# Decay attention and a gated convolution on one core: all 707 pieces of work in another written order

## The chip, the core and the metric

The kernel runs on one core of a Trainium2 chip. The metric is device time in microseconds of one execution. The kernel before takes 206.38 us, the median of three runs (206.31 to 206.44). A core has five engines with a queue of instructions each, and the queues run in order: TensorE (PE; its weight loads are listed apart as PEld), VectorE (DVE), ScalarE (ACT), GpSimd (POOL) and SyncE (SP), which here issues every transfer.

## The reference

Two stages. The first is a causal linear attention with a decay per head, over 4 batches, 8 heads, 768 positions and a head width of 64; `lam` holds the decay of each head. In blocks of positions, with a running state of 64x64 per head:

```
intra = (q_b @ k_b^T) * lam^(i-j), lower triangle
out_b = intra @ v_b + (q_b * lam^(i+1)) @ state
state = lam^block * state + (k_b * lam^(block-1-i))^T @ v_b
```

The second takes the result as `x` (4 batches, 768 tokens, 512 channels):

```
gate_pre[t] = sum over k < 5 of conv_w[k] * x[t - 4 + k]      (per channel)
out = (sigmoid(gate_pre) * (x @ w_val)) @ w_out
```

`q`, `k`, `v` and `lam` are float32; `w_val`, `conv_w` and `w_out` arrive as float64.

## The kernel before

A **chunk** is 128 positions of two batches, all heads; there are 12, numbered 0 to 11, and 0 to 5 share one running state, as do 6 to 11. Two chunks are a **unit** for the convolution. The work is cut into 707 **pieces**, each a few instructions on one engine, that the functions below register with `plan.add`. The order in which pieces are emitted, and so the order of every engine's queue, is written out by hand in the string `ORDER` (from line 32). `Plan.run` walks through it and emits each piece. What follows a colon in `ORDER` names the buffers that the piece takes: `u0` to `u3` are four banks of PSUM that most results pass through, `lq0` to `lq2` and `lv0` to `lv2` are the landing places of loads. Semaphores that a layer below derives from the data keep the result right in any order that `Plan.run` accepts; the order alone decides who waits.

```
    def run(self):
        done = set()
        for piece in ORDER.split():
            name, _, takes = piece.partition(":")
            k = self.at[name]
            assert k not in done and done.issuperset(self.work[k][3]), name
            done.add(k)
            self.takes = takes.split(",") if takes else []
            self.work[k][2]()
```

The names that the later sections use, with chunk number i (or unit n), engine and line:

- On the transfer queue: `ld.i.0` loads q and k of a chunk transposed (1 MB, `lq`, L337), `ld.i.2` loads v and k (1 MB, `lv`, L337), `wv.u` and `wo.u` load halves of the two weight matrices as raw 64-bit words (1 MB each, L355), `cv` the convolution's weights (20 KB, L370), `o...` stores a result (256 KB, L851).
- Weights are turned from float64 into a high and a low float32 part by integer steps: `.e .n .s .w .v` on DVE (L261 to L293), `.r .m .h` on ACT, `.l` on POOL (L303).
- Attention on PE: `s.i.u` scores (L460 and L470), `ia.i.u` scores times v (`xp`, L525 and L510), `in.i.u` q times state (also into `xp`, L536 and L547), `st.i` k times v (L564 and L572). These are short matmuls of 64 or 128 columns, 32 to 64 instructions a piece. Beside them: `m.i.b.u` multiplies scores by the decay mask (DVE, L483 and L490), `kd.i` scales k, `up.i` updates the state (DVE, L581), `fd.i` decays it (POOL, L584), `x.i` copies `xp` out of PSUM (ACT, L634), `xh.i` and `xl.i` split it into high and low parts.
- Second stage on PE: `v.i.f` and `V.n.f` are the value products (`vp`, L732), 12 matmuls of 256 columns for one chunk or of 512 for a whole unit, and `p.i.b.j.u` the output products (`op`, L841), 6 matmuls of 512 columns. `t.` are the five taps of the convolution (ACT then DVE, L704 and L706), `sg` the sigmoid, `pb.i.u` copies `vp` out of PSUM (ACT, L773), `ap`, `hh`, `hl` multiply and split, `ev` copies the output out of PSUM (ACT, L848).
- `f.0` (L206) is a matmul of zeros that nothing reads, there to keep PE occupied.

Loads wait on SP for their landing place: `ld.5.2` for example takes `lv1`, which chunk 3 holds until `ia.3.1` and `st.3` have read it.

Of the kernel before, what the change touches and what calls it, by code (L numbers as in the profile page):

```python
# [33 lines left out]
ld.1.2:lv1 wv.1:g1 m.0.0.1:A1 m.0.1.1 ia.0.1 f.0:u2 wv.0.0.e:val0 ld.2.0:lq2 wv.0.0.n ld.4.0:lq0 cv wv.0.0.r
wv.0.1.e:val1 ld.2.2:lv2 wv.0.0.m:u3 wv.0.0.s wv.0.0.w xh.0:xs0 wv.0.0.v wo.0:hs0 xl.0 st.0:u2 qd.1.1:qd0 up.0.0
wv.0.1.r wv.0.0.h s.1.0:s0 m.1.1.0:A0 s.1.1:u0,u1 m.1.0.0 dc wv.0.0.l v.0.0:u3 m.1.0.1:A1 x.0:x0 qd.1.0 ld.3.0:lq1
fd.0.0 kd.1.0 wo.1:hs1 m.1.1.1 wv.0.1.n ia.1.0:xp0 ia.1.1 wv.0.1.m:u2 ld.4.2:lv0 wv.1.0.e:val2 in.1.0 st.1:u0 wv.0.1.s
wv.0.1.w wv.0.1.v wv.0.1.h ld.3.2:lv1 wv.1.0.n s.2.0:s0 wv.1.1.e:val3 s.2.1:u1,u2 up.1.0 xh.1 wv.0.1.l v.0.1
m.2.0.0:A0 m.2.1.0 wv.1.0.m:u0 xl.1 wv.1.0.w wv.1.0.r hi.0 pb.0.0:val0 m.2.0.1:A1 wv.1.0.s cv.e qd.2.0:qd1 wv.1.0.v
qd.2.1 wv.1.1.n x.1 wv.1.1.r cv.r s.4.0:s0 cv.n v.1.0:u3 v.1.1 wv.1.0.h wv.1.1.s wv.1.1.m:u0 m.2.1.1 wv.1.1.w wv.1.1.v  # L40
ia.2.0:xp0 ia.2.1 wv.1.0.l cv.m m.4.1.0:A0 kd.2.0 wv.1.1.h fd.1.0 wo.0.0.n:val1 cv.s in.2.0 x.2:x1 pb.1.0:val2
wv.1.1.l m.4.0.0 st.2:u1 wo.0.0.e wo.0.0.r up.2.0 qd.4.0:qd0 cv.w cv.v xh.2:xs1 wo.1.1.e:val3 t.0.0.0:u2,g0 s.3.0:s0
xl.2.0 wo.0.0.m:u0 v.0.2:u3 m.3.0.0:A1 ld.6.2:lv2 v.0.3 pb.0.1 t.0.0.1 kd.3.0 t.0.0.2 xl.2.1 t.0.0.3 wo.0.0.w qd.4.1
ld.5.0:lq2 wo.0.0.s t.0.0.4 v.1.2:u1 sg.0.0 qd.3.1:qd1 v.1.3 v.2.2:u3 v.2.3 pb.1.1 wo.1.1.n fd.2.0 wo.0.0.v m.3.1.0
wo.1.1.m:u2 wo.1.1.r ld.6.0:lq0 st.3:u0,u1 wo.0.0.h qd.3.0 ia.3.0:xp0 in.3.0 wo.1.1.w wo.1.1.s wo.1.1.v wo.0.0.l hi.1
s.5.0:s0 kd.4.0 v.2.0:u2 up.3.0 in.3.1 wo.0.1.e:val1 wo.0.1.r fd.3.0 wo.1.1.h wo.0.1.n wo.0.1.m:u0 wo.0.1.s wo.1.1.l
up.3.1 fd.3.1 ia.3.1 v.2.1 x.3 xh.3 xl.3.1 ia.4.0:xp0 t.0.1.0:u1 ld.5.2:lv1 wo.0.1.w xl.3.0 pb.2.0:val3 m.5.1.0:A1
m.5.0.0 wo.0.1.v pb.2.1 wo.0.1.h wo.0.1.l s.6.0:s0 st.4:u0,u2 qd.5.1:qd1 kd.6.0 t.0.1.1 t.0.1.2 t.0.1.3 in.4.0 up.4.0
fd.4.0 t.0.1.4 sg.0.1 v.3.0:u3 kd.5.0 v.3.2:u0 qd.5.0 in.4.1 ia.4.1 ld.7.2:lv0 t.0.3.0:u1 t.0.3.1 up.4.1 t.0.3.2
x.4:x2 t.0.3.3 t.0.2.0:u2 kd.5.1 v.3.3 pb.3.1:val1 t.0.2.1 t.0.2.2 xh.4:xs0 ld.7.0:lq1 ia.5.0:xp0 in.5.0 t.0.2.3  # L50
fd.4.1 st.5:u0 up.5.0 v.3.1 pb.3.0 t.0.3.4 xl.4.1 in.5.1 sg.0.3 t.0.2.4 ap.1.0 ap.0.0 sg.0.2 ap.1.1 xl.4.0
wo.1.0.e:val2 wo.1.0.r v.4.0:u0 v.4.2:u3 wo.1.0.n wo.1.0.m:u1 ap.0.1 v.4.1 wo.1.0.s hh.1.1:hs0 wo.1.0.w pb.4.0:val0
hh.1.0 hl.1.1 wo.1.0.v m.6.1.0:A0 v.4.3 m.6.0.0 t.1.1.0:u2,g1 t.1.1.1 wo.1.0.h ia.5.1 st.6:u0,u1 up.6.0 x.5 s.7.0:s0
ia.6.0:xp0 hl.1.0 p.1.1.0.0:u0 t.1.1.2 hh.0.1:hs1 hh.0.0 t.1.1.3 pk.6 wo.1.0.l p.1.1.0.1 pb.4.1 qd.6.1:qd0 t.1.1.4
qd.6.0 t.1.3.0:u3 sg.1.1 t.1.3.1 t.1.3.2 t.1.3.3 t.1.3.4 ev.1.1.0:o0 o.1.1.0 xh.5 in.6.1 hi.2 ia.6.1 p.1.0.0.0:u2
fd.6.0 x.6:x0 t.1.0.0:u0 hl.0.0 sg.1.3 hl.0.1 p.1.0.0.1 up.6.1 ld.11.2:lv1 t.1.0.1 t.1.0.2 t.1.0.3 t.1.0.4
p.0.1.0.0:u1 ev.1.0.0:o1 p.0.1.0.1 t.1.2.0:u3 m.7.0.0:A1 t.1.2.1 t.1.2.2 t.1.2.3 m.7.1.0 sg.1.0 xl.5.0 p.0.0.0.0:u2
p.0.0.0.1 xl.5.1 v.5.0:u0 ld.8.0:lq2 t.1.2.4 ev.0.1.0:o2 o.1.0.0 xh.6:xs1 qd.7.0:qd1 t.2.3.0:u1,g0 v.5.1 ap.3.0
ld.8.2:lv2 ev.0.0.0:o0 sg.1.2 pb.5.0:val2 ap.3.1 ap.2.0 qd.7.1 kd.7.1 ia.7.0:xp0 in.7.0 kd.7.0 ap.2.1 hh.2.1:hs0
st.7:u2,u3 fd.6.1 v.5.2:u0 v.5.3 hh.2.0 t.2.3.1 t.2.3.2 up.7.0 s.8.0:s0 in.7.1 t.2.3.3 t.2.1.0:u2 t.2.3.4 hh.3.0:hs1  # L60
ia.7.1 hh.3.1 hl.2.0 sg.2.3 pb.5.1 p.2.0.0.0:u1 t.2.0.0:u0 t.2.1.1 ld.9.2:lv0 t.2.1.2 t.2.0.1 fd.7.0 up.7.1 hl.2.1
t.2.0.2 t.2.0.3 kd.8.0 p.2.0.0.1 ev.2.0.0:o1 t.2.0.4 sg.2.0 p.2.1.0.0:u3 kd.8.1 t.2.2.0:u1 t.2.1.3 p.2.1.0.1 t.2.1.4
o.2.0.0 sg.2.1 m.8.0.0:A0 o.0.0.0 t.2.2.1 t.2.2.2 t.2.2.3 t.2.2.4 ev.2.1.0:o1 o.0.1.0 ap.4.0 ap.5.0 ld.9.0:lq0 hl.3.1
hi.3 hl.3.0 x.7 p.3.0.0.0:u0 p.3.0.0.1 p.3.1.0.0:u2 t.3.0.0:u3,g1 xh.7 p.3.1.0.1 o.2.1.0 ia.8.0:xp0 sg.2.2 ap.4.1
t.3.0.1 hh.4.0:hs0 t.3.0.2 t.3.0.3 qd.8.1:qd0 fd.7.1 qd.8.0 in.8.0 ev.3.0.0:o0 hl.4.0 hh.4.1 hl.4.1 ev.3.1.0:o2
t.3.0.4 st.8:u1,u0 up.8.0 xl.6.0 ap.5.1 p.4.0.0.0:u2 m.8.1.0 t.3.1.0:u1 xl.7.1 p.4.0.0.1 fd.8.0 in.8.1 t.3.1.1 t.3.1.2
ia.8.1 t.3.1.3 ev.4.0.0:o1 o.4.0.0 ld.10.0:lq1 s.9.0:s0 m.9.1.0:A1 p.4.1.0.0:u2 sg.3.0 x.8:x1 p.4.1.0.1 xl.6.1
hh.5.0:hs1 t.3.2.0:u3 ev.4.1.0:o1 up.8.1 t.3.2.1 t.3.1.4 xl.7.0 V.3.0:u0 t.3.2.2 sg.3.1 m.9.0.0 t.3.3.0:u2 hl.5.0
t.3.2.3 t.3.2.4 sg.3.2 t.3.3.1 t.3.3.2 V.3.1:u1 ld.11.0:lq2 ld.10.2:lv2 V.3.2:u3 qd.9.1:qd1 qd.9.0 qd.10.1:qd0 t.3.3.3
kd.9.1 fd.8.1 kd.9.0 apw.3.0 xh.8:xs0 hhw.3.0:hs0 kd.11.1 o.3.0.0 t.3.3.4 apw.3.1 hhw.3.1 ia.9.0:xp0 hlw.3.0:val1  # L70
hlw.3.1 in.9.0 st.9:u0,u1 sg.3.3 hh.5.1 apw.3.2 hhw.3.2 V.3.3:u2 up.9.0 fd.9.0 kd.11.0 kd.10.0 in.9.1 ia.9.1 s.10.0:s0
apw.3.3 hhw.3.3 qd.10.0 hlw.3.2:val3 p.7.0.0.0:u0 hlw.3.3 x.9 hi.4 t.4.1.0:u3,g1 hl.5.1 p.5.1.0.0:u2 p.5.1.0.1
ev.5.1.0:o0 m.10.0.0:A0 up.9.1 p.7.0.0.1 t.4.1.1 o.5.1.0 t.4.1.2 t.4.1.3 t.4.1.4 sg.4.1 kd.10.1 ia.10.0:xp0 fd.9.1
st.10:u1,u2 xh.9 in.10.0 up.10.0 m.10.1.0 ev.7.0.0:o0 o.7.0.0 qd.11.0:qd1 p.6.1.0.0:u3 p.6.1.0.1 in.10.1 ia.10.1
o.4.1.0 x.10:x2 t.4.0.0:u0 xh.10:xs1 s.11.0:s0 qd.11.1 ev.6.1.0:o0 o.6.1.0 fd.10.0 up.10.1 st.11:u1 m.11.0.0:A1
fd.10.1 t.4.0.1 t.4.0.2 ia.11.0:xp0 in.11.0 up.11.0 m.11.1.0 o.3.1.0 xl.9.0 p.6.0.0.0:u2 xl.9.1 t.4.0.3 t.4.0.4
p.6.0.0.1 ev.6.0.0:o1 sg.4.0 p.7.1.0.0:u3 t.4.2.0:u1 t.4.2.1 in.11.1 ia.11.1 x.11 t.4.2.2 xh.11 t.4.2.3 p.7.1.0.1
t.4.2.4 xl.8.1 xl.8.0 t.4.3.0:u2 sg.4.2 t.4.3.1 t.4.3.2 V.4.0:u0 apw.4.0 t.4.3.3 V.4.2:u1 t.4.3.4 hhw.4.0:hs0
ev.7.1.0:o0 sg.4.3 hlw.4.0:val0 V.4.1:u3 apw.4.1 apw.4.2 hhw.4.1 hlw.4.1 hi.5 t.5.1.0:u2,g0 t.5.1.1 hhw.4.2 V.4.3:u0
apw.4.3 hlw.4.2:val2 hhw.4.3 p.5.0.0.0:u3 t.5.1.2 p.5.0.0.1 p.9.0.0.0:u1 xl.10.0 hlw.4.3 p.9.0.0.1 t.5.1.3 t.5.1.4  # L80
t.5.3.0:u0 ev.5.0.0:o2 o.5.0.0 sg.5.1 ev.9.0.0:o2 p.8.0.0.0:u3 p.8.0.0.1 o.9.0.0 xl.11.0 xl.10.1 xl.11.1 V.5.1:u2
t.5.3.1 t.5.0.0:u1 t.5.3.2 t.5.3.3 t.5.3.4 sg.5.3 ev.8.0.0:o2 t.5.0.1 t.5.0.2 t.5.0.3 t.5.0.4 sg.5.0 p.9.1.0.0:u0
t.5.2.0:u3 o.8.0.0 apw.5.1 hhw.5.1:hs1 t.5.2.1 t.5.2.2 p.9.1.0.1 ev.9.1.0:o2 t.5.2.3 t.5.2.4 sg.5.2 o.7.1.0 V.5.0:u1
hlw.5.1:val1 V.5.3:u0 apw.5.0 o.9.1.0 apw.5.3 hhw.5.3 hlw.5.3:val3 p.8.1.0.0:u2 p.8.1.0.1 V.5.2:u3 hhw.5.0 ev.8.1.0:o0
o.8.1.0 hlw.5.0 p.10.1.0.0:u0 o.6.0.0 apw.5.2 hhw.5.2 hlw.5.2 p.11.1.0.0:u1 p.11.0.0.0:u2 p.11.0.0.1 ev.11.0.0:o2
o.11.0.0 p.11.1.0.1 ev.11.1.0:o0 o.11.1.0 p.10.1.0.1 ev.10.1.0:o1 o.10.1.0 p.10.0.0.0:u3 p.10.0.0.1 ev.10.0.0:o2
o.10.0.0 p.11.1.1.0:u2 p.11.1.1.1 ev.11.1.1:o0 o.11.1.1
"""


# [812 lines left out]
```

## Time and profile before

| | |
|---|---|
| median of 3 runs | 206.38 us (206.31 to 206.44) |
| the profiled execution's own time | 206.52 us |
| its span, from the first to the last instruction | 204.7 us |
| PE, PEld busy | 97%, 84% of the span |
| DVE, ACT, POOL busy | 75%, 56%, 56% |
| TensorE clock granted | full (mean 1.00) |
| transfers | 36.15 MB, mean 177 GB/s; 360 to 429 GB/s in the slices from about 5 to 46 us |

The span is 1.8 us shorter than the execution; that share lies outside the program's instructions. PE's busy share is a modelled one, since matmuls overlap; the chain of waits and the waits by engine tell more. The first 45 us are the dense part: the loads of the weights and of the first six chunks stream without a break, and DVE and ACT turn the weights into two parts beside the attention's own work.

### The profile page before, as it was taken

The numbers are of one execution on the slowest core, as the hardware profiler recorded it, in microseconds if no ns is written. First come the engines' busy times: TensorE is split into PE (matmuls) and PEld (weight loads), VectorE is DVE, ScalarE is ACT, GpSimd is POOL, SyncE is SP. The second block draws the span as 40 slices with busy tenths as digits, with TensorE's granted clock in tenths as the row PEclk, the third lists the DMA queues.
The fourth block names the chain that finished last, engine by engine and source line by source line (L and its number), as shares of the span: only waits on it lengthen the run. The fifth ranks groups of instructions, "written<-read, shape, count | busy, mean of one in ns | idle before, by whom it ended". The sixth has DMA issues, their size and how long they took to land.

```text
span 204.7 us, 7451 instructions
## 1 busy us (share of the span) xinstructions
PE 197.6 (97%) x3312; PEld 171.6 (84%) x3312; DVE 154.1 (75%) x240; ACT 114.3 (56%) x218; POOL 115.4 (56%) x113
## 2 busy tenths in 40 slices
...
GB/s 175 426 429 419 422 424 423 421 360 27 195 51 362 8 3 118 373 232 3 297 297 29 203 400 122 3 3 152 8 106 0 0 3 102 102 51 14 93 127 78
DMA packets 7952, 36.15 MB, mean 177 GB/s; under 512 B 1136, under 2 KB 1392, under 8 KB 4336
## 3 DMA queue, kind: packets, MB, share of 16 engines
...
q8 instruction: 26, 0.43, 0.9%
q14 instruction: 6, 0.05, 0.1%
...
## 4 chain that ended last, share of the span: by engine, by line
PE 87%; DMA 9%; SPq 2%; issue 0%; ACT 0%; ACTq 0%
PE op L841 33%; PE vp L732 33%; DMA lq<-in_qkv 9%; PE xp L510 5%; PE s L470 5%; PE xp L547 5%; PE st L572 4%; SPq L337 1%; PE xp L525 1%; PE s L460 1%; PE st L564 1%; PE xp L536 1%; SPq L355 0%; PE so L460 0%; ACT o L848 0%
## 5 line engine op out<-in xcount | busy, mean ns | idle before, releaser
L706 DVE SCALAR_TENSOR_TENSOR acc<-x,conv_sb,acc 128x512 f32<-128x512 f32 x96 | 71.5, 753 | 7.8 <-ACT acc L704 5.7
L732 PE MATMUL vp<-x_hi,wv_hi 128*128 128x256 f32 (+1 forms) x144 | 47.1, 327 | 0.0
L732 PE MATMUL vp<-x_hi,wv_lo 128*128 128x256 f32 (+1 forms) x144 | 45.9, 319 | 0.3 <-POOL wv_lo L303 0.3
L732 PE MATMUL vp<-x_lo,wv_hi 128*128 128x256 f32 (+1 forms) x144 | 45.8, 318 | 0.0
L841 PE MATMUL op<-wo_hi,hs 128*128 128x512 f32 x96 | 30.4, 398 | 0.0
L848 ACT COPY o<-op 128x512 f32<-128x512 f32 (+1 forms) x25 | 14.3, 570 | 28.5 <-PE op L841 24.2
L732 PEld LDWEIGHTS vp<-x_hi,wv_hi 128*128 128x128 f32 x144 | 27.3, 190 | 2.8
L732 PEld LDWEIGHTS vp<-x_hi,wv_lo 128*128 128x128 f32 x144 | 27.4, 190 | 2.4 <-POOL wv_lo L303 0.5
L732 PEld LDWEIGHTS vp<-x_lo,wv_hi 128*128 128x128 f32 x144 | 27.4, 190 | 1.9
L677 POOL TENSOR_TENSOR x_lo<-x,x_hi 128x512 fp32r<-128x512 f32 x20 | 25.8, 1311 | 4.7 <-ACT x_hi L666 4.7
L584 POOL TENSOR_TENSOR sdec<-state,qdec_c 128x512 f32<-128x512 f32 x17 | 18.4, 1080 | 9.2 <-DVE state L581 9.2
L814 POOL TENSOR_TENSOR hs<-g,hs 128x512 fp32r<-128x512 f32 x12 | 15.4, 1294 | 13.6 <-ACT hs L803 13.6
L420 POOL TENSOR_TENSOR qd<-lq,qdec_c 128x512 f32<-128x512 f32 (+1 forms) x18 | 22.6, 1272 | 0.0
L841 PEld LDWEIGHTS op<-wo_hi,hs 128*128 128x128 f32 x96 | 17.7, 188 | 4.0
L841 PE MATMUL op<-wo_hi,h_hi 128*128 128x512 f32 (+1 forms) x52 | 20.0, 385 | 0.0
L841 PE MATMUL op<-wo_hi,h_lo 128*128 128x512 f32 (+1 forms) x52 | 19.6, 377 | 0.0
L704 ACT ACTIVATE acc<-x,conv_sb 128x512 f32<-128x512 f32 x24 | 16.7, 696 | 5.1 <-DVE state L581 3.6
L841 PE MATMUL op<-wo_lo,h_hi 128*128 128x512 f32 (+1 forms) x52 | 19.5, 375 | 0.0
L841 PE MATMUL op<-wo_lo,hs 128*128 128x512 f32 x48 | 18.9, 393 | 0.0
L803 ACT CAST h_hi<-vp 128x512 fp32r<-128x512 f32 x12 | 6.9, 587 | 21.0 <-DVE vp L778 21.0
L581 DVE TENSOR_TENSOR state<-st,sdec 128x512 f32<-128x512 f32 x17 | 11.7, 688 | 8.8 <-PE xp L547 6.4
L778 DVE TENSOR_TENSOR vp<-vp,g 128x512 f32<-128x512 f32 x12 | 8.3, 698 | 11.9 <-PE vp L732 11.9
...
## 6 DMA issues: line engine op xcount, KB each, us to landing
lq<-in_qkv SPq DMA_DIRECT2D x12, 1024.0 KB, 7.8
lv<-in_qkv SPq DMA_DIRECT2D x12, 1024.0 KB, 8.0
...
w_raw<-in_w_val SPq DMA_DIRECT2D x2, 1024.0 KB, 12.6
w_raw<-in_w_out SPq DMA_DIRECT2D x2, 1024.0 KB, 17.6
...
lam_bc<-in_lam SPq DMA_DIRECT2D x1, 4.0 KB, 1.6
```

The source lines that it names most:

```text
L420: nc.gpsimd.tensor_tensor(out=s["qd"][:, hs, ms], in0=lds[i]["qT"][:, u].rearrange("p h (m i) -> p h m i", m=2)[:, :, ms], in1=qdec[:, hs, ...
L470: nc.tensor.matmul(sp[b][rows(m), k, :], t["kT"][rows(b), u, h, ms], t["qT"][rows(b), u, h, ms], start=True, stop=True,)
L510: nc.tensor.matmul(s["xp"][rows(hh), b ^ m, b, g, :], lds[i]["v"][rows(m), b, h * D : (h + 1) * D], s["A"][rows(m), b, h, :], start=b == 0 ...
L581: nc.vector.tensor_tensor(out=state, in0=s["st"][m], in1=sdec, op=ALU.add)
L584: nc.gpsimd.tensor_tensor(out=sdec, in0=state, in1=qdec_c[:, :, n - 1 : n].to_broadcast([P, H, D]), op=ALU.mult)
L677: nc.gpsimd.tensor_tensor(out=s["x_lo"][:, ts], in0=s["x"][:, ts], in1=s["x_hi"][:, ts].bitcast(F32), op=ALU.subtract)
L704: nc.scalar.mul(to, src, w)
L706: nc.vector.scalar_tensor_tensor(out=to, in0=src, scalar=w, in1=to, op0=ALU.mult, op1=ALU.add)
L732: nc.tensor.matmul(to, w[:, ct, fs], xx[:, ct], start=n_mm == 0, stop=n_mm == 3 * NT - 1)
L814: (nc.vector if direct else nc.gpsimd).tensor_tensor(out=to, in0=x["h", j, fs], in1=x["to", j, fs].bitcast(F32), op=ALU.subtract)
L841: nc.tensor.matmul(s["op", b, j][:, cols], hh, w[:, ft, cols], start=ft == 0 and n == 0, stop=ft == NT - 1 and n == 2,)
L848: nc.scalar.copy(s["o", b, j][:, cols], s["op", b, j][:, cols])
```

## The change

Only the string `ORDER` changes; no piece, engine, size or buffer count does, and every engine issues as many instructions as before. The new order keeps the same outline. The string's first line, before and after:

```
-ld.0.0:lq0 dm.0 dm.1 qe ld.0.2:lv0 kd.0.0 s.0.0:s0 kd.0.1 m.0.0.0:A0 s.0.1:u0,u1 m.0.1.0 ia.0.0:xp0 wv.0:g0 ld.1.0:lq1
...
+dm.0 dm.1 dc ld.0.0:lq0 qe f.0:u0 ld.0.2:lv0 kd.0.1 s.0.1:u0,u1 m.0.1.1:A0 s.0.0:s0 wv.0:g0 kd.0.0 m.0.0.1 m.0.1.0:A1
...
```

Three places, as the built programs list their instructions.

The transfer queue (SP) near its start, from the first half of `w_val` on, before and then after. `lq` and `lv` are loads of chunks, `w_raw` of weights, `conv_raw` of the convolution's weights.

```order
L355 DMA w_raw<-in_w_val 128x2048
L337 DMA lq<-in_qkv 128x2048
L337 DMA lv<-in_qkv 128x2048
L355 DMA w_raw<-in_w_val 128x2048
L337 DMA lq<-in_qkv 128x2048 x2
L370 DMA conv_raw<-in_conv_w 128x40
L337 DMA lv<-in_qkv 128x2048
L355 DMA w_raw<-in_w_out 128x2048
```

```order
L355 DMA w_raw<-in_w_val 128x2048
L337 DMA lq<-in_qkv 128x2048
L337 DMA lv<-in_qkv 128x2048
L370 DMA conv_raw<-in_conv_w 128x40
L355 DMA w_raw<-in_w_val 128x2048
L337 DMA lq<-in_qkv 128x2048 x2
L355 DMA w_raw<-in_w_out 128x2048
L337 DMA lv<-in_qkv 128x2048
```

The convolution's weights (`cv`) now stand ahead of the second half of `w_val` and of `ld.2.0`, and the first half of `w_out` (`wo.0`) ahead of `ld.2.2`.

DVE at the start, before and then after: the masks of chunk 0 (`A`), then the first steps on the weights (`w_em`, `w_v`).

```order
L483 TENSOR_TENSOR A<-s,mask_c 128x512 x2
L483 TENSOR_TENSOR A<-so,mask_c 128x512 x2
L261 TENSOR_SCALAR w_em<-w_raw 128x512
L268 TENSOR_SCALAR w_em<-w_raw 128x512
L261 TENSOR_SCALAR w_em<-w_raw 128x512
L281 SCALAR_TENSOR_TENSOR w_em<-w_raw,w_em 128x512
```

```order
L483 TENSOR_TENSOR A<-so,mask_c 128x512 x2
L483 TENSOR_TENSOR A<-s,mask_c 128x512 x2
L261 TENSOR_SCALAR w_em<-w_raw 128x512 x2
L268 TENSOR_SCALAR w_em<-w_raw 128x512 x2
L281 SCALAR_TENSOR_TENSOR w_em<-w_raw,w_em 128x512
```

The second half of the heads is masked first, and a fourth step on the weights (`wv.0.1.n`) stands ahead of the sign step of the first block (`wv.0.0.s`).

PE around chunk 4, between `v.2.1` and the next value products, before and then after: `ia.4.0`, `s.6.0`, `st.4`, `in.4.0` are the four short pieces.

```order
L732 MATMUL vp<-x_hi,wv_lo 128x256
L510 MATMUL xp<-A,lv 64x64 x16
L470 MATMUL s<-lq 64x64 x32
L572 MATMUL st<-lv 64x64 x32
L547 MATMUL xp<-qd,state 64x64 x16
L732 MATMUL vp<-x_hi,wv_hi 128x256
```

```order
L732 MATMUL vp<-x_hi,wv_lo 128x256
L510 MATMUL xp<-A,lv 64x64 x16
L547 MATMUL xp<-qd,state 64x64 x16
L572 MATMUL st<-lv 64x64 x32
L470 MATMUL s<-lq 64x64 x32
L732 MATMUL vp<-x_hi,wv_hi 128x256
```

The same four stand there; `in.4.0` and `st.4` come ahead of `s.6.0`. A little earlier, the run `st.3`, `ia.3.0`, `in.3.0`, `s.5.0` becomes `ia.3.0`, `st.3`, then the product `v.2.3`, then `in.3.0`, `s.5.0`, `in.3.1`; `v.2.0` now stands between `in.3.1` and `ia.3.1`, which were neighbours. `f.0` moves from behind `ia.0.1` to the head of PE's queue, ahead of the first scores.

## Rows read from the trace of the kernel before

**Rows 1.** The page: span, and busy time by engine.
```profile
span 204.7 us, 7451 instructions
PE 197.6 (97%) x3312; PEld 171.6 (84%) x3312; DVE 154.1 (75%) x240; ACT 114.3 (56%) x218; POOL 115.4 (56%) x113
```

**Rows 2.** Instructions in time, PE, to 24 us: start, length, what, idle before and releaser.
```profile
10.76 1.12 PE L206 MATMUL fill<-zero 128*128 128x512 f32 x2
12.04 1.15 PE L564 MATMUL st<-lv 128*64 128x64 f32 x32
13.64 1.16 PE L460 MATMUL s<-lq 64*128 64x128 f32 x16 [0.45 <-DMA lq<-in_qkv]
20.78 1.15 PE L564 MATMUL st<-lv 128*64 128x64 f32 x32
22.45 1.16 PE L460 MATMUL s<-lq 64*128 64x128 f32 x16 [0.52 <-DMA lq<-in_qkv]
```

**Rows 3.** Instructions in time, DVE, from 8 to 12 us.
```profile
8.62 1.28 DVE L483 TENSOR_TENSOR A<-so,mask_c 128x512 f32<-128x512 f32 x2
11.51 0.42 DVE L268 TENSOR_SCALAR w_em<-w_raw 128x512 int32<-128x512 int32 x1
```

**Rows 4.** The chain that ended last: start, length, what; here the issue of ld.2.0.
```profile
4.34 18.07 DMA lq<-in_qkv
```

**Rows 5.** Instructions in time, SP: issues of ld.1.2 and of ld.5.2.
```profile
3.32 0.45 SPq L337 DMA_DIRECT2D lv<-in_qkv  x1
50.01 0.33 SPq L337 DMA_DIRECT2D lv<-in_qkv  x1
```

**Rows 6.** DMA issues from 3.2 to 3.4 us: KB each, us to landing.
```profile
lv<-in_qkv SPq DMA_DIRECT2D x1, 1024.0 KB, 14.4
```

**Rows 7.** The chain that ended last, from 49 to 58 us.
```profile
49.90 1.63 PE vp L732 x12
51.53 0.62 PE xp L510 x32
52.15 0.99 PE s L470 x53
53.14 0.10 issue
53.24 0.39 PE s L470 x10
55.08 3.06 PE vp L732 x24
```

**Rows 8.** The chain that ended last, from 71 to 74 us.
```profile
71.09 0.62 PE xp L510 x32
71.71 0.93 PE st L572 x64
72.64 0.93 PE s L470 x64
73.58 0.47 PE xp L510 x32
```

**Rows 9.** DMA queues of the page, then those of 50.9 to 51 us: packets, MB, share.
```profile
q8 instruction: 26, 0.43, 0.9%
...
q8 instruction: 1, 0.02, 59.1%
```

**Rows 10.** The same from 46.4 to 46.5 us.
```profile
q8 instruction: 1, 0.02, 89.3%
```

**Rows 11.** Instructions in time near chunks 3 and 4, PE, DVE and ACT.
```profile
45.60 0.65 PE L547 MATMUL xp<-qd,state 64*64 64x64 f32 x32
46.38 0.69 DVE L581 TENSOR_TENSOR state<-st,sdec 128x512 f32<-128x512 f32 x1 [0.64 <-POOL x L641]
49.97 1.08 ACT L634 COPY x<-xp 128x512 f32<-128x512 f32 x2 [0.66 <-PE xp L510]
51.07 1.05 ACT L666 CAST x_hi<-x 128x1024 fp32r<-128x1024 f32 x1
52.65 1.06 ACT L773 COPY val<-vp 128x512 f32<-128x512 f32 x2
```

More of the change, by code (lines that the diff above doesn't have):

```diff
@@ L32 @@
 ORDER = """
-ld.0.0:lq0 dm.0 dm.1 qe ld.0.2:lv0 kd.0.0 s.0.0:s0 kd.0.1 m.0.0.0:A0 s.0.1:u0,u1 m.0.1.0 ia.0.0:xp0 wv.0:g0 ld.1.0:lq1
[L34 to L87, printed above, removed]
+dm.0 dm.1 dc ld.0.0:lq0 qe f.0:u0 ld.0.2:lv0 kd.0.1 s.0.1:u0,u1 m.0.1.1:A0 s.0.0:s0 wv.0:g0 kd.0.0 m.0.0.1 m.0.1.0:A1
@@ new lines @@
+m.0.0.0 ia.0.0:xp0 ld.1.0:lq1 ld.1.2:lv1 ia.0.1 wv.0.0.e:val0 cv wv.1:g1 wv.0.1.e:val1 wv.0.0.n qd.1.1:qd0 wv.0.1.n
+wv.0.0.r wv.0.0.s ld.2.0:lq2 ld.4.0:lq0 wo.0:hs0 wv.0.0.m:u2 wv.0.0.w wv.0.0.v xh.0:xs0 xl.0 ld.2.2:lv2 wv.0.0.h
+wv.0.0.l wv.0.1.r st.0:u3 x.0:x0 qd.1.0 s.1.1:u0,u1 up.0.0 s.1.0:s0 fd.0.0 v.0.0:u2 ld.3.0:lq1 m.1.0.0:A1 m.1.1.0
+m.1.0.1:A0 ia.1.0:xp0 m.1.1.1 wo.1:hs1 cv.e ld.4.2:lv0 ia.1.1 in.1.0 wv.0.1.m:u3 kd.1.0 st.1:u0 wv.0.1.s wv.0.1.w
+wv.0.1.v wv.0.1.h ld.3.2:lv1 cv.n cv.m wv.1.0.n:val2 wv.1.1.e:val3 up.1.0 wv.0.1.l s.2.0:s0 wv.1.0.e xh.1 xl.1
```

49 lines of the change are left out of this document (added).

## The prediction

> **What bounds the kernel now.** I read the page's busy times first. PE is busy for 197.6 of 204.7 us [rows 1]; the other engines have at least 50 us to spare, so what counts is PE's stretch from its first real matmul to its last, and in it the moments in which PE stands still or runs at less than its usual pace. Next the instructions in time on PE. Up to 22.45 us the loads set the pace: `s.1.0` waits 0.45 us for `ld.1.0`, `s.2.0` 0.52 us for `ld.2.0` [rows 2], which was issued at 4.34 and landed 18.07 us later, at 22.41 [rows 4]. From then on the chain of waits consists of PE alone, piece on piece, and a wait is visible only as a piece that takes longer than its like. There is one place of that kind. The four short pieces around chunk 4 start at 51.53 and the next product at 55.08, so they take 3.55 us [rows 7]. The same kinds (`ia`, `st`, `s`, `ia`) around chunk 6 take 0.62 + 0.93 + 0.93 + 0.47 = 2.95 us [rows 8]. So 0.60 us is lost there, nearly all in `s.6.0`: 0.99 + 0.10 + 0.39 = 1.48 us, where `s.7.0` takes 0.93. The chain marks a part of it as issue, time in which no semaphore is waited for.
>
> What else PE fetches at that moment is in the DMA queues: PE's instructions come in 26 packets, 0.43 MB, so 16 KB each [rows 9]. One of them starts between 50.9 and 51.0 us, right behind the issue of `ld.5.2` at 50.01 into a queue that had run empty [rows 5], and lasts 0.591 x 16 x 0.1 = 0.95 us, to about 51.9. The hole in `s.6.0` ends at 53.24, 1.3 us after that packet. I read the hole as an instruction page that came late; the rows show the coincidence, not the cause.
>
> **The change part by part.** Work and durations stay, so PE's sum changes only by its starts, its switches and its waits. I count against the profiled execution (206.52 us, of which 204.7 are the span) and carry the difference over to the median of 206.38.
>
> *Start, to 22.45 us: +0.05.* Three edits, all behind a load. `f.0` (1.12 us) [rows 2] moves ahead of the first scores, which wait for their load anyhow. In its place comes a wait: DVE now masks the second half first, so `ia.0.0` needs all four masks, which are done at 9.90 [rows 3]. `ia.0.0` and `ia.0.1` need about 2 us, so `st.0` again starts at about 12.0 and ends at 13.2; `s.1` waits for its load until 13.64 either way. Cover 0.4 us. One more weight step (0.42 us) [rows 3] ahead of `wv.0.0.s` makes the low part of the first weight block up to 0.4 us later, and with it `v.0.0` and all up to `st.1`, which ended at 21.93 [rows 2]: 22.3 at the latest, still under the landing at 22.41. What remains is the landing itself: the 20 KB of `cv` now lie ahead of `ld.2.0`. From the landing of `ld.1.2` (3.32 + 14.4 = 17.7) [rows 5, 6] to 22.41 two transfers of 1,024 KB take 4.7 us, 2.35 each, so 20 KB cost 0.05 us by bytes. Bounds 0 and, as its rows are small, 0.3; I take 0.05. `wo.0` ahead of `ld.2.2` puts that load 2.35 us later, near 29.8; its first reader on PE is due about 30.2. I cost it at nothing; if the cover were gone, each 0.1 us that it is late costs 0.1.
>
> *Switches between short and long matmuls: +0.35.* `v.2.3` is cut out of a row of products and `v.2.0` put between `in.3.1` and `ia.3.1`, so from 22 us on PE has one more stretch of products and one more of short pieces. A product of its own takes 1.63 us, two in a row 3.06, so 1.43 for one more in a row [rows 7]: 0.20 a stretch. A short `xp` piece takes 0.62 next to a product and 0.47 among short ones [rows 8]: 0.15. Bounds 0 (if the other places regain it) and 0.4.
>
> *The hole around chunk 4: -0.60.* The packet is asked for by PE's place in its own stream. Ahead of `ia.3.1` stands now the long `v.2.0` in place of the short `in.3.1`, so the request can go out during a product that lasts 1.6 us, more ahead of `ld.5.2`, whose issue still waits for `ia.3.1`. I count the hole and the small wait with it as gone. Bounds 0 and -0.60; nearer to -0.60, since a request 0.3 us earlier is enough.
>
> *Two new waits: +0.10 and +0.15.* `in.3.1` follows `s.5.0` at once, and needs `up.3.0`, which needs `in.3.0`. In the trace `in.3.0` starts at 45.60 and `up.3.0` is done at 47.07, 1.47 us later [rows 11]; PE gets to `in.3.1` after 0.47 + 0.93 = 1.40. With the hand-over between engines some 0.1 us. And `st.4` writes a bank that `pb.2.1` empties, which ACT does behind `x.3` and `xh.3`: from the end of `ia.3.1` at 49.90 these end at 52.1, and one copy of 1.06 / 2 more [rows 11] makes 2.7 us; PE's way from there is `v.2.1`, `ia.4.0`, `in.4.0`, 1.63 + 0.62 + 0.47 = 2.72. A tie, with a hand-over on ACT's side: 0.15. In the order before, `s.6.0` lay between. Bounds 0 and 0.3 each. Behind a waiting `st.4` stands PE's queue alone.
>
> *Everything behind 56 us: 0.* The outline is kept, PE's last pieces are again two halves of the last output, and the tail behind them (copy, store) is the same.
>
> Sum: 0.05 + 0.35 - 0.60 + 0.10 + 0.15 = +0.05, so 206.4.
>
> **A rule that speaks against the hole's cause.** The rows show 26 packets of 16 KB and, once, PE short of instructions [rows 7, 9]. The Trainium skill, "Runtime: NRT & Kernel Launch", section "Instruction fetch mechanics", says that the sequencer fetches the next block of 256 instructions while it executes the current one, and that crossing a block is mostly hidden. The block size agrees with the packets here; the hole, if it is one of fetching, does not agree with hidden. By that rule the hole has another cause and stays as it is: that is the third rival below.
>
> **The rivals.**
>
> *Faster, 205.9.* `ld.1.2` landed 4.1 us after `ld.1.0` (13.6, by the wait of `s.1.0`) [rows 2], where the next two took 2.35 each: 1.7 us of the load stream went astray. If that does not recur, `ld.2.0` is there at 20.7, and `s.2.0` starts when PE gets there, about 22.15: -0.30, and the 0.05 of `cv` with it. If also the two new waits do not show: -0.25. Sum +0.05 - 0.35 - 0.25 = -0.55. For it: both waits are near ties. Against: the packets of PE's instructions and the loads meet again in the same first 20 us.
>
> *Slower, 207.2.* The late page strikes harder. The four short pieces still stand in a row and `ld.5.2` is still issued when `ia.3.1` ends. PE reaches the point at which it ran dry (53.24 less a hole of 0.3) after the same work, some 0.4 us later by the switches and the wait of `in.3.1`, so near 53.3; the packet must end 1.3 us ahead of that, by 52.0 us. Where packets meet other traffic they last longer: 0.893 x 1.6 = 1.43 us at 46.4 us against 0.95 [rows 9, 10]. A packet that starts as late as before (50.95), half a microsecond later for the load ahead of it, and lasts 1.43, ends at 52.9 and costs 0.9, of which `st.4` hides its 0.15. Sum +0.05 + 0.75 = +0.8. It decides as soon as the packet ends later than 52.0. For it: the places are close. Against: the earlier request.
>
> *The hole stays, 206.7.* 53 of the 64 instructions of `s.6.0` should take 53/64 x 0.93 = 0.77 us, and the 54th came 1.09 after the first: 0.32 is the hole without the rest. It stays as it is, since the packet goes out as late as before, and the sum is +0.05 + 0.32 = +0.37, less a little that the wait at `st.4` shares with it. The rule above gives the same.
>
> **How the numbers follow.** Forecast 206.4 (its own range 206.0 to 206.8): chance 0.54. Faster rival 0.20, slower rival 0.16, hole stays 0.10. A measurement of this kernel tells about 0.2% from no change, so 205.97 and 206.79 are the borders. Of the forecast 0.02 lies beyond each border, of the last rival 0.02 beyond the upper one. Faster 0.20 + 0.02 = 0.22, slower 0.16 + 0.02 + 0.02 = 0.20, same 0.58. The range 205.8 to 207.2 leaves out about a third of the faster rival and half of the slower one, 0.15.
>
> **What would show it.** Right: `s.2.0` starts at 22.3 to 22.6 with a wait for its load; the four short pieces around chunk 4 take about 3.0 us plus a wait at `st.4` of at most 0.3, with no piece of the chain marked issue; PE's last matmul ends within 0.4 us of 201.7. Wrong: `s.2.0` at 22.2 or earlier (faster rival); an instruction packet that ends later than 52.0 and a hole behind it (slower rival); a new wait anywhere behind 56 us, where I expect none, which would make the whole sum wrong.

## The result and the profile after

The changed kernel takes 208.01 us (median of 4 runs, 207.96 to 208.24). The kernel before, run beside it on the same chip, takes 206.41 (206.31 to 206.45). The ratio is 1.0081, with a 95% interval of 1.0069 to 1.0093. So the change costs 1.6 us, where 206.4 was forecast and 207.2 was the upper end of the range.

The head of the page of the changed kernel, answering to [rows 1]:

```profile
span 206.2 us, 7454 instructions
...
PE 198.6 (96%) x3312; PEld 171.9 (83%) x3312; DVE 153.0 (74%) x240; ACT 114.8 (56%) x218; POOL 114.8 (56%) x113
...
PE 86%; DMA 8%; DVE 2%; issue 1%; ACT 1%; SPq 1%; POOL 1%; ACTq 0%
```

The span grew by 1.5 us and PE's busy time by 1.0 (197.6 to 198.6). The last line, the shares of the chain of waits, has two entries to look into. DMA stood at 9% before too, but there all of it was the load of `s.2.0` at the start; of the 8% here the page puts 4% down to `out<-o`, the store of a result. And "issue" has gone from 0% to 1%.

The chain from 22 us on, answering to [rows 2] (columns: start, length, what):

```profile
22.40 1.16 PE s L460 x16
...
24.46 1.64 PE vp L732 x12
26.10 0.90 issue
27.00 1.16 PE s L470 x64
```

`s.2.0` starts at 22.40, 0.05 us ahead of before and inside the forecast 22.3 to 22.6, though not with the forecast wait: its load has landed at 22.27, just when TensorE is through with `st.1`. But `s.4.0` starts at 27.00, 0.90 us after TensorE was free, where before it started at 26.06 with no wait. The view calls this gap "issue", and the view of instructions in time names the last product as what `s.4.0` waited for. Neither tells the cause: what `s.4.0` needs is its bank, and that is free when VectorE has masked both halves of `s.2.0` (`m.2.0.0`, `m.2.1.0`). VectorE and GpSimd at that moment, instructions in time:

```profile
22.39 0.69 DVE L581 TENSOR_TENSOR state<-st,sdec 128x512 f32<-128x512 f32 x1 [0.64 <-PE st L564]
22.99 1.52 DVE L261 TENSOR_SCALAR w_em<-w_raw 128x512 int32<-128x512 int32 x1
24.43 1.28 DVE L672 TENSOR_TENSOR x_lo<-xp,x_hi 128x512 fp32r<-128x512 f32 x2
25.63 1.27 DVE L483 TENSOR_TENSOR A<-s,mask_c 128x512 f32<-128x512 f32 x2
...
22.95 2.71 POOL L413 TENSOR_TENSOR qd<-lq,qdec_c 128x512 f32<-128x512 f32 x2
```

The two masks (L483) end at 26.90, and `s.4.0` starts 0.1 us later. Ahead of them stand `wv.1.0.e` (L261) and `xl.1` (L672), which the change has moved there. And `wv.1.0.e` takes 1.52 us. In the kernel before, the same step ran with GpSimd idle and took 0.43:

```profile
20.00 0.43 DVE L261 TENSOR_SCALAR w_em<-w_raw 128x512 int32<-128x512 int32 x1 [1.02 <-DMA w_raw<-in_w_val]
```

There the same two masks ended at 24.95, 1.1 us before TensorE came to `s.4.0`:

```profile
23.66 1.29 DVE L483 TENSOR_TENSOR A<-s,mask_c 128x512 f32<-128x512 f32 x2
...
26.06 1.16 PE L470 MATMUL s<-lq 64*64 64x64 f32 x64
```

Around chunk 4, answering to [rows 7]:

```profile
52.92 0.62 PE xp L510 x32
53.55 0.47 PE xp L547 x32
54.01 1.13 PE st L572 x61
55.15 0.01 PE s L470
55.15 0.05 PE st L572 x3
55.20 0.93 PE s L470 x63
56.14 1.87 PE vp L732 x14
```

The four short pieces now take 56.14 - 52.92 = 3.22 us instead of 3.55. The hole in `s.6.0` is gone; `st.4` takes 0.26 more than its like [rows 8], 0.15 of it in one gap between two of its instructions.

The second loss lies behind 96 us (the same view, the pieces that matter):

```profile
97.75 0.33 SPq L337
...
98.13 7.43 DMA out<-o
...
105.64 0.60 ACT o L848
...
106.28 3.04 PE op L841 x12
```

The store `o.0.0.0` was issued at 98.13, right behind the load `ld.9.2` (97.75), and landed only 7.43 us later. The copy `ev.2.0.0` needs the buffer that it empties, and `p.3.0.0.0` needs the bank which that copy empties. TensorE stands still for 0.32 us.

In the starts of TensorE's pieces against the kernel before, the delay is -0.05 at `s.2.0`, +0.94 at `v.1.0`, +1.06 at `v.3.3` (60 us), +1.45 at `p.4.1.0.0` (116 us) and +1.53 at the end (203.22 against 201.69).

### The profile page after: what moved, and what is told of

Same layout as the page of the kernel before. It is cut to its first block, busy times and chain, and to the rows that moved or that the text cites. A ratio compares the mean times of both kernels' runs of the same rounds, so it can differ in the third digit from the quotient of the medians.

```text
span 206.2 us, 7454 instructions
## 1 busy us (share of the span) xinstructions
PE 198.6 (96%) x3312; PEld 171.9 (83%) x3312; DVE 153.0 (74%) x240; ACT 114.8 (56%) x218; POOL 114.8 (56%) x113
## 4 chain that ended last, share of the span: by engine, by line
PE 86%; DMA 8%; DVE 2%; issue 1%; ACT 1%; SPq 1%; POOL 1%; ACTq 0%
PE vp L732 34%; PE op L841 29%; PE xp L510 5%; PE xp L547 5%; DMA w_raw<-in_w_val 4%; PE s L470 4%; PE st L572 4%; DMA out<-o 4%; PE xp L525 2%; PE st L564 1%; PE xp L536 1%; POOL wv_lo L303 1%; SPq L337 1%; PE s L460 1%; ACT o L848 0%
## 5 line engine op out<-in xcount | busy, mean ns | idle before, releaser
L420 POOL TENSOR_TENSOR qd<-lq,qdec_c 128x512 f32<-128x512 f32 (+1 forms) x18 | 22.6, 1263 | 0.0
L711 ACT ACTIVATE g<-acc 128x512 f32<-128x512 f32 x24 | 14.4, 599 | 9.8 <-DVE acc L706 9.6
L581 DVE TENSOR_TENSOR state<-st,sdec 128x512 f32<-128x512 f32 x17 | 11.7, 687 | 7.3 <-PE st L572 3.6
```

Source lines behind the costliest of these rows:

```text
L420: nc.gpsimd.tensor_tensor(out=s["qd"][:, hs, ms], in0=lds[i]["qT"][:, u].rearrange("p h (m i) -> p h m i", m=2)[:, :, ms], in1=qdec[:, hs, ...
L581: nc.vector.tensor_tensor(out=state, in0=s["st"][m], in1=sdec, op=ALU.add)
L711: nc.scalar.activation(xu[un]["g"][:, ct].rearrange("p u (b i) -> p b u i", b=NB2), xu[un]["acc", ct].rearrange("p b (u i) -> p b u i", u= ...
```

## Experiments

All edits but three are in the order string alone (the two runs with an extra GpSimd step and the measurement at the end have code as well). The diffs show the pieces that move, cut out of their lines. The theory (A): VectorE comes late at 27 us because one of its steps was slowed by GpSimd's work, and the store comes late at 105 us because of the load ahead of it; each of the two makes TensorE wait. Against it stood (B) TensorE short of instructions at 27 us, and (C) the place of `xl.1` alone. Each ratio is to runs of the kernel before on the same chip.

**GpSimd held still during `wv.1.0.e`.** One GpSimd step more, a copy of one column of that step's result, ahead of `qd.2.1`:

```diff
- wv.1.0.e xh.1 xl.1 qd.2.1:qd1 qd.2.0
+ wv.1.0.e xh.1 xl.1 gate qd.2.1:qd1 qd.2.0
+ add("gate", "POOL", lambda: nc.gpsimd.tensor_copy(gate, s["e"][:, 0:1]), [t_e], bufs)
```

> The changed kernel with one instruction more: GpSimd copies one column of the result of wv.1.0.e before it begins qd.2.1, so that GpSimd stands still while VectorE runs wv.1.0.e; all orders are as they were. Theory A (the instruction took 1.52 us because GpSimd was working beside it): it takes 0.42 to 0.45 us, m.2.1.0 ends near 25.8, s.4.0 starts near 26.1 with no wait, and 0.9 us of the 1.6 come back: about 207.1. Theory B (the 0.90 us that the chain marks as issue is TensorE short of instructions): s.4.0 still starts near 27.0, 208.0. Theory C (only the place of xl.1 ahead of the masks, in VectorE's order, makes them late): wv.1.0.e stays at 1.5 us, s.4.0 near 27.0, 208.0.

Measured: 207.86 us, ratio 1.0066 (1.0054 to 1.0079). VectorE, GpSimd and TensorE in time:

```profile
23.11 0.42 DVE L261 TENSOR_SCALAR w_em<-w_raw 128x512 int32<-128x512 int32 x1
23.44 1.28 DVE L672 TENSOR_TENSOR x_lo<-xp,x_hi 128x512 fp32r<-128x512 f32 x2
24.64 1.28 DVE L483 TENSOR_TENSOR A<-s,mask_c 128x512 f32<-128x512 f32 x2
...
23.59 0.19 POOL L310 COPY gate<-w_em 128x1 int32<-128x1 int32 x1 [0.49 <-DVE w_em L261]
23.73 2.54 POOL L413 TENSOR_TENSOR qd<-lq,qdec_c 128x512 f32<-128x512 f32 x2
...
26.42 1.16 PE L470 MATMUL s<-lq 64*64 64x64 f32 x64
```

The mechanism is shown: in the same place of the same order the step takes 0.42 us with GpSimd idle, and `s.4.0` has no wait (the whole stretch lies 0.41 us later here, since `ld.2.0` landed later). B and C fall. But the time moved little: the forecast 207.1 missed. TensorE won 0.99 us at `s.4.0`, so that it was 0.58 us ahead in spite of the late start, and `p.3.0.0.0` then waited 0.81 us instead of 0.32, since the store landed at 105.47, nearly when it did in the changed kernel (105.56). The second wait took back half of what the first had given, and the late start most of the rest.

**`xl.1` behind the masks, as before the change.**

```diff
- xl.1 qd.2.1:qd1 qd.2.0 wv.1.0.r m.2.0.0:A1 s.2.1:u1,u3 v.0.1 wv.1.0.m:u0 wv.1.1.r m.2.1.0
+ qd.2.1:qd1 qd.2.0 wv.1.0.r m.2.0.0:A1 s.2.1:u1,u3 v.0.1 wv.1.0.m:u0 wv.1.1.r m.2.1.0 xl.1
```

> The changed kernel with xl.1 put behind m.2.0.0 and m.2.1.0 on VectorE, as it stood before; wv.1.0.e stays ahead of them, beside GpSimd's qd.2.1. Theory A: wv.1.0.e still takes 1.5 us, but m.2.1.0 ends near 25.7, just ahead of the 26.1 at which TensorE is free: s.4.0 starts on time, about 207.1. So neither of the two would have cost anything alone. Theory B (short of instructions): no change, 208.0.

Measured: 207.59 us, ratio 1.0061 (1.0049 to 1.0074). `wv.1.0.e` takes 1.49 us, the masks end at 25.58, `s.4.0` is on time. So the slow step alone, without `xl.1` in the queue, doesn't delay `s.4.0`; it takes both. But the forecast 207.1 missed here too, since the slow step isn't free: `ia.2.0` waited 0.31 us for `x.1`, which ScalarE ran behind the late `wv.1.0.h`, and `in.8.1` waited 0.18 near 115 us. TensorE is 0.45 us ahead at the end.

**The stores ahead of the load.**

```diff
- ld.9.2:lv0
+ o.0.0.0 o.0.1.0 ld.9.2:lv0
```

(the two stores no longer stand behind it)

> The changed kernel with the stores o.0.0.0 and o.0.1.0 issued ahead of the load ld.9.2 instead of behind it. If the store that waits behind the load holds up ev.2.0.0 and with it p.3.0.0.0: the store lands by about 93 us, the 0.32 us in front of p.3.0.0.0 go, and with the little behind it about 207.65. If the wait for the buffer is only where another delay shows (the products of chunk 3 late on VectorE or ScalarE): the stall stays at 0.2 to 0.3, 208.0. s.4.0 starts near 27.0 either way.

Measured: 207.44 us, ratio 1.0049 (1.0035 to 1.0063). Issues to DMA in the changed kernel at 98 us, then the two stores in this one at 89.8 us (KB each, us to landing):

```profile
out<-o SPq DMA_DIRECT2D x1, 256.0 KB, 7.4
```

```profile
out<-o SPq DMA_DIRECT2D x2, 256.0 KB, 2.5
```

The wait at `p.3.0.0.0` is gone, and TensorE gains 0.41 us between 97 and 109 us. `s.4.0` still waits; it starts at 26.86, 0.14 us earlier than in the changed kernel since VectorE came to its steps that much earlier in this run, which is the rest of the gain.

**Both.** The two edits together:

```diff
- wv.1.0.e xh.1 xl.1 qd.2.1:qd1 qd.2.0
+ wv.1.0.e xh.1 xl.1 gate qd.2.1:qd1 qd.2.0
- ld.9.2:lv0
+ o.0.0.0 o.0.1.0 ld.9.2:lv0
```

> The changed kernel with both edits of the first runs: GpSimd stands still during wv.1.0.e, and the stores o.0.0.0 and o.0.1.0 are issued ahead of ld.9.2. Theory A (two stalls one behind the other; the stall at p.3.0.0.0 ends when the store lands, 105.5, whenever TensorE gets there, so it takes back what is won at s.4.0): the gains now add, 0.95 + 0.45 = 1.4 us: 206.6, though the two alone gave 0.15 and 0.57. Rival D (what is won at s.4.0 is lost at any of several later waits, not at this store): about 207.3, with a new stall behind 60 us.

Measured: 206.89 us, ratio 1.0033 (1.0021 to 1.0046). The 0.15 and 0.57 of the expectation are differences between medians of two series; by the ratios the two edits alone gave 0.15% and 0.32%, both together 0.48%, and with intervals of 0.12% either way the times don't tell a plain sum from more than a sum. The trace does: counted from `s.2.0`, TensorE wins 0.99 us at `s.4.0` and 0.39 at `p.3.0.0.0`, and keeps both, and there is no new stall (rival D is out). Of the 0.29 us above 206.6, 0.20 are in the start: `s.2.0` began that much later than in the changed kernel.

**Without the extra step.** `wv.1.0.e` and `wv.1.1.e` change places on VectorE, and the latter goes behind the masks; stores ahead of the load:

```diff
- wv.1.1.e:val3 up.1.0 wv.0.1.l s.2.0:s0 wv.1.0.e xh.1 xl.1
+ wv.1.0.e up.1.0 wv.0.1.l s.2.0:s0 xh.1 xl.1
- m.2.1.0 pb.0.0:val0
+ m.2.1.0 wv.1.1.e:val3 wv.1.1.r pb.0.0:val0
```

> The changed kernel with the stores ahead of ld.9.2, and on VectorE the places of wv.1.0.e and wv.1.1.e exchanged and wv.1.1.e put behind m.2.1.0; no instruction is added. Theory A: wv.1.0.e runs before GpSimd begins, 0.42 us; xl.1 ends near 24.3, m.2.1.0 near 25.6, no stall at s.4.0, 206.5. If the place in VectorE's order and not GpSimd made the step long: wv.1.0.e short, but m.2.1.0 still late, s.4.0 near 27.0, 207.5.

Measured: 206.64 us, ratio 1.0017 (1.0008 to 1.0026). The step takes 0.42 us, TensorE's last product ends at 201.73. So the two waits make up 0.64% of the 0.81%, 1.3 of the 1.6 us.

**The mirror image: only those two steps moved in the kernel before.**

```diff
- wv.1.0.e:val2 in.1.0
+ in.1.0
- up.1.0 xh.1
+ up.1.0 wv.1.0.e xh.1
- m.2.0.0:A0 m.2.1.0 wv.1.0.m:u0 xl.1
+ xl.1 m.2.0.0:A0 m.2.1.0 wv.1.0.m:u0
```

> The kernel before with only two steps of VectorE moved as the change moves them: wv.1.0.e behind up.1.0, xl.1 ahead of m.2.0.0. GpSimd runs wv.0.1.l from about 23.1 to 24.4 there. Theory A: wv.1.0.e starts near 23.55 beside it and takes 0.8 to 1.5 us, m.2.1.0 ends near 27.2 and s.4.0 waits 1.1 us; the store at 98 us isn't in the way in this order: 207.4 to 207.7. Theory B (s.4.0 was short of instructions for another reason): 206.4.

Measured: 207.06 us, ratio 1.0035 (1.0023 to 1.0048).

```profile
22.89 1.17 DVE L261 TENSOR_SCALAR w_em<-w_raw 128x512 int32<-128x512 int32 x1
...
22.44 1.28 POOL L303 TENSOR_TENSOR wv_lo<-w_em,wv_hi 128x512 fp32r<-128x512 f32 x1 [3.75 <-ACT wv_hi L299]
...
26.55 1.16 PE L470 MATMUL s<-lq 64*64 64x64 f32 x64 [0.64 <-PE vp L732]
```

The two steps make `s.4.0` wait there too: 0.71 us, and the time grows by 0.8. The size was forecast too high (207.4 to 207.7). The step's own 1.17 us lie within the 0.8 to 1.5 of the expectation, with GpSimd's step begun 0.45 us ahead of it as expected; but VectorE came to it at 22.89 instead of 23.55, so the masks ended at 26.45 and not near 27.2.

**The page behind the hole.** In the kernel before, `in.3.1` ahead of `v.2.0`:

```diff
- v.2.0:u2 up.3.0 in.3.1
+ up.3.0 in.3.1 v.2.0:u2
```

> The kernel before with one step moved: in.3.1 ahead of the product v.2.0 instead of behind it, all else as it was. If the hole in s.6.0 is an instruction page that is asked for too late (the request goes out during the four short pieces, behind ld.5.2): the page is asked for about 1 us earlier, s.6.0 takes 0.93 to 1.1 instead of 1.48 us, in.3.1 may wait 0.06 us for up.3.0, about 206.0. If the hole is something else (fetching is hidden; a wait of s.6.0 itself): it stays, 206.4.

Measured: 206.48 us, ratio 1.0004 (0.9995 to 1.0012). The instruction packet now starts at 49.92, 1.0 us earlier, and ends at 50.84 (DMA queues from 49.9 to 50 us, read as in [rows 9]: 0.575 x 1.6 = 0.92 us):

```profile
q8 instruction: 1, 0.02, 57.5%
```

`s.6.0` takes 0.93 us with no gap. So the gap behind the 53rd instruction of `s.6.0`, 0.31 us in the kernel before, was a late page. It was not all of the 0.55 us that `s.6.0` lost: some 0.2 lay at its first instructions, which started right behind VectorE's masks of `s.5.0` (they end at 52.05 in the kernel before and at 51.42 here, where `up.3.1` runs earlier). And behind it `st.4` waited 0.40 us and `in.3.1` waited 0.13: the hole had covered a wait of `st.4` for the copy `pb.2.0`, and the time stayed, where 206.0 had been forecast. The next run takes that wait away as well, with `pb.2.0` ahead of `t.0.1.0` on ScalarE:

```diff
- t.0.1.0:u1 ld.5.2:lv1 wo.0.1.w xl.3.0 pb.2.0:val3
+ pb.2.0:val3 t.0.1.0:u1 ld.5.2:lv1 wo.0.1.w xl.3.0
```

> The kernel before with in.3.1 ahead of v.2.0, as in the earlier run, and pb.2.0 ahead of t.0.1.0 on ScalarE. In that run the packet started at 49.92 instead of 50.9 and s.6.0 had no hole, but st.4 waited 0.40 us for the copy pb.2.0. If that copy is what the hole had covered: it ends near 52.6 instead of 53.2, st.4 waits under 0.1, and the gain shows: 206.1. If st.4 waits for another bank or the page comes late again: 206.45.

Measured: 206.42 us, ratio 1.0008 (0.9999 to 1.0017): no gain. The chain:

```profile
51.50 0.62 PE xp L510 x32
52.12 1.06 PE s L470 x63
53.19 0.02 PE st L572 x3
53.21 0.04 PE s L470
53.25 0.88 PE st L572 x60
```

`st.4` doesn't wait any more (0.93 us in all), but the packet came at 50.42 this time, 0.5 us later than with the same order of TensorE in the run ahead, and 0.09 us of the hole is back. The three runs agree: the packet ends at 51.89, 51.34 and 50.84, the hole is 0.31, 0.09 and 0 us, and the first instruction behind it starts 1.35 and 1.46 us after the packet in the two that have one. The rest is lost in the two products behind it, `v.3.0` and `v.3.2`, together 0.17 us longer than in the run ahead, most of it ahead of the first instruction of `v.3.2` at 56.19. A packet ends at 55.2, but 1.35 us behind it would be near 56.6, so a late page isn't shown to be the cause there; it stays open.

**The split product put back.** On top of the run at 206.64, `v.2.3` beside `v.2.2`:

```diff
- v.2.2:u3 ia.3.0:xp0
+ v.2.2:u3 v.2.3 ia.3.0:xp0
```

> The changed kernel without its two stalls (stores ahead of ld.9.2, wv.1.0.e ahead of GpSimd's work, as in the run at 206.64), and with the product v.2.3 put back beside v.2.2. If a stretch of products more costs what the prediction said (0.20 for the product, 0.15 for the short piece behind it): 0.3 us less, 206.35. If the change of order costs nothing there (other pieces regain it, or in.3.1 now waits as long as is won): 206.6.

Measured: 206.30 us, ratio 0.9991 (0.9975 to 1.0007). TensorE is 0.33 us ahead from `v.2.0` on, 0.29 at the end. The price of the split, 0.35, was right. With the 1.3 us of the two waits it makes up the 1.6 us, within the intervals.

**A version from these.** On top of that, `pb.2.1` ahead of `xh.3` on ScalarE:

```diff
- xh.3 m.5.0.0:A0 m.5.1.0 t.0.1.2 v.2.1 pb.2.1:val3
+ m.5.0.0:A0 m.5.1.0 t.0.1.2 v.2.1 pb.2.1:val3 xh.3
```

> The same as the run with v.2.3 put back, and on ScalarE the copy pb.2.1 ahead of xh.3, so that st.4 finds its bank free: the 0.15 us at st.4 go, if nothing behind xh.3 is late for it: 206.2, level with the kernel before. If TensorE then comes to the next instruction page too early, as with the packet at 54.3 in the runs of the kernel before: 206.35.

Measured: 206.07 us, ratio 0.9981 (0.9966 to 0.9997). It is the only version whose interval lies below the kernel before, and barely: the medians differ by 0.1% (206.07 against 206.28), and the runs of the kernel before beside it scatter from 206.0 to 208.1. In its chain the four short pieces take 2.96 us, as their like at chunk 6 (2.95 [rows 8]), so all of the 0.26 us at `st.4` was the wait for `pb.2.1`:

```profile
51.52 0.62 PE xp L510 x32
52.14 0.47 PE xp L547 x32
52.61 0.93 PE st L572 x64
53.54 0.93 PE s L470 x64
54.48 2.11 PE vp L732 x16
```

**Which steps GpSimd slows.** A measurement behind the last step of the changed kernel: four forms on VectorE, three of each, alone and then beside a row of GpSimd products.

```diff
+ nc.vector.tensor_scalar(out=tv, in0=ti[:, :, 1], scalar1=20, scalar2=0x7FF, op0=ALU.logical_shift_right, op1=ALU.bitwise_and)
+ nc.vector.scalar_tensor_tensor(out=tv, in0=ti[:, :, 1], scalar=-(1 << 31), in1=tv, op0=ALU.bitwise_and, op1=ALU.bitwise_or)
+ nc.vector.tensor_tensor(out=fw, in0=fw, in1=fv, op=ALU.mult)
+ nc.vector.tensor_copy(fw, fv)
+ nc.gpsimd.tensor_tensor(out=ta, in0=ta, in1=tb, op=ALU.mult)
```

> The changed kernel with a measurement put behind its last step: on VectorE three each of the int32 TENSOR_SCALAR of L261, the int32 SCALAR_TENSOR_TENSOR of L281, an f32 TENSOR_TENSOR and an f32 COPY, all 128x512, first with GpSimd idle, then again beside a row of 13 GpSimd products of 128x512. If GpSimd slows only some forms: TENSOR_SCALAR 0.42 alone and 0.8 to 1.5 beside it, TENSOR_TENSOR and SCALAR_TENSOR_TENSOR 0.68 both times or a little more; the copy tells whether the fast forms as a whole are hit. If what counted in this case was int32 or the strided operand and not the form: SCALAR_TENSOR_TENSOR slows like TENSOR_SCALAR. If it was something else beside it in time (a transfer landing): 0.42 both times.

Measured (VectorE alone, with the first two of the three COPYs, then VectorE and GpSimd beside each other):

```profile
198.69 1.29 DVE L876 TENSOR_SCALAR probe<-probe 128x512 int32<-128x512 int32 x3
200.01 2.14 DVE L878 SCALAR_TENSOR_TENSOR probe<-probe,probe 128x512 int32<-128x512 int32 x3
202.19 2.15 DVE L880 TENSOR_TENSOR probe<-probe 128x512 f32<-128x512 f32 x3
204.37 0.89 DVE L882 COPY probe<-probe 128x512 f32<-128x512 f32 x2
...
207.77 3.22 DVE L876 TENSOR_SCALAR probe<-probe 128x512 int32<-128x512 int32 x3
211.03 4.97 DVE L878 SCALAR_TENSOR_TENSOR probe<-probe,probe 128x512 int32<-128x512 int32 x3
216.03 4.97 DVE L880 TENSOR_TENSOR probe<-probe 128x512 f32<-128x512 f32 x3
221.04 4.17 DVE L882 COPY probe<-probe 128x512 f32<-128x512 f32 x3
...
207.93 19.73 POOL L888 TENSOR_TENSOR probe<-probe 128x512 f32<-128x512 f32 x13 [0.81 <-DVE probe L886]
```

All four are hit. One TENSOR_SCALAR or COPY takes 0.43 us alone and 1.37 beside GpSimd, one SCALAR_TENSOR_TENSOR or TENSOR_TENSOR 0.69 and 1.63: 0.94 more each. (The first of the three TENSOR_SCALARs began 0.16 us ahead of GpSimd's row and took 0.42; the other two 1.37.) None of the expectations had TENSOR_TENSOR slow, and the form isn't what decides: in the kernel itself the masks (L483) and the state update (L581), TENSOR_TENSORs with an operand in PSUM, take 0.67 to 0.69 us with GpSimd busy or not. The probe's operands all lie in SBUF, and so do those of the SCALAR_TENSOR_TENSOR of L281, which took 1.24 us at 48.81 in the changed kernel, behind a GpSimd step begun 0.37 us earlier. That the place of the operands decides is read from these rows; no run moved an operand alone.

What also counts is who begins first. In the changed kernel the same form as `wv.1.0.e` ran at 33.88 in 0.42 us, though a GpSimd step began 0.23 us into it.

## Why the prediction was wrong, point by point

**The step that failed.** "From then on the chain of waits consists of PE alone", and with it "Work and durations stay": the sum has no term for VectorE between 22.45 and 27 us. The change puts `wv.1.0.e` and `xl.1` ahead of the masks that free the bank of `s.4.0`, and this moved row wasn't looked at. With the durations of quiet rows it would have just fitted: the run with GpSimd held still has the masks done at 25.91, 0.1 us before 26.01, when TensorE would need the bank with the changed kernel's start (22.40 + 3.61; in that run itself it came at 26.42). So naming the wait wasn't enough, the 0.42 us had to be doubted too, and the trace of before had the row for that, the same step beside a GpSimd step:

```profile
33.15 1.31 DVE L261 TENSOR_SCALAR w_em<-w_raw 128x512 int32<-128x512 int32 x1
```

```profile
32.89 1.28 POOL L303 TENSOR_TENSOR wv_lo<-w_em,wv_hi 128x512 fp32r<-128x512 f32 x1 [1.04 <-ACT wv_hi L299]
```

There nobody waited for it. The missing term is +0.99 us: the step took 1.52 us and not 0.42, and together with `xl.1` it put the end of the masks at 26.90. A slow rival of this kind wasn't among the three either: the slower one that was named, a later page, did not happen (the packet ended at 51.06 and not behind 52.0).

The runs agree with a rule of the Trainium skill ("SBUF — State Buffer", section "Who interferes with whom"): copies and tensor_scalar in their fast modes, and instructions with two SBUF inputs against a GpSimd step that reads SBUF, share a port pair with GpSimd, and the one that issues first blocks the other for its whole instruction. By the same section of the Trainium skill a VectorE instruction with at most one SBUF input, outside those modes, doesn't contend. By these two rules the 0.43 to 1.37, the 0.69 to 1.63, the masks at 0.67 to 0.69 and the 0.42 of the step that began ahead of GpSimd's are all what one expects; no run here looks at the ports themselves.

**"Everything behind 56 us: 0" failed as well.** It was argued from the outline of TensorE's order; the order of SP's queue was not followed there. `ev.2.0.0` now takes the buffer of `o.0.0.0`, and that store stands behind `ld.9.2`: +0.32 us at `p.3.0.0.0` and +0.39 by 116 us. The prediction had named such a wait as what would make the whole sum wrong.

**The start, +0.05, measured -0.05.** Right within the scatter, and partly by luck: the 20 KB of `cv` don't show (`ld.2.0` landed at 22.27, 0.14 us earlier than before), and what set the start was the other half of the sum, the weight steps, by which `st.1` ended at 22.27 instead of 21.93 ("22.3 at the latest"). The landing of `ld.2.0` alone moves `s.2.0` between runs by more (22.3 to 22.8 in the versions of the changed kernel).

**Switches, +0.35, measured +0.34** (`v.2.2` to `v.2.1`: 9.09 us against 8.65, less 0.10 for the wait of `in.3.1`), and 0.33 when `v.2.3` was put back. Right, and all of it is `v.2.3`: the other half of that term, `v.2.0` in its new place, cost nothing.

**The hole, -0.60, measured -0.59** (-0.33 for the four pieces, which contain the 0.26 of `st.4`). The cause was right for the 0.31 us of the page; most of the rest was the wait at the head of `s.6.0`. The third rival (it stays) is out; the packet came at 49.99 instead of 50.94. The Trainium skill's "mostly hidden" ("Runtime: NRT & Kernel Launch", "Instruction fetch mechanics") does not hold for this one of the 26 packets; behind 27 us the trace of before shows no second gap of this size.

**New waits, +0.10 and +0.15, measured +0.10 and +0.26.** `in.3.1` takes 0.57 us where its like takes 0.47: right. The wait of `st.4` came from the copy that was named, and was sized too low, within its bounds.

Measured sum to 60 us: -0.05 + 0.99 + 0.34 - 0.59 + 0.10 + 0.26 = +1.05; then +0.39 and 0.09 more spread over the rest: 1.53 at the end of TensorE's last product, 1.60 in the medians. Without the two terms that were missing, the forecast of +0.05 stands beside 0.15; its misses at the start and at `st.4` cancel.
